# Idle matmuls in two bursts, and a re-ordered start: one change to a fused linear-attention and MLP kernel

## The chip, the cores and the metric

The kernel runs on one core of one Trainium2 chip. The metric is the device time of one execution in microseconds (us). Three runs of the kernel before took 603.48 us (median), from 602.2 to 605.39. Inside the core five engines work side by side, each with its own queue in program order: TensorE (PE in the profile; PEld is its weight load), VectorE (DVE), ScalarE (ACT), GpSimd (POOL) and SyncE (SP, which here only issues DMAs). An engine whose next instruction waits for another engine or for a DMA stands, with everything behind it in its queue.

## The reference

The attention part is a delta rule over 4 x 8 heads, 768 tokens and head size 48; its output goes through a two-layer MLP.

```
for t in range(S):
    kt, vt, bt = (k_n[:, :, t], v[:, :, t], beta[:, :, t, None])
    y[:, :, t] = np.einsum('bhd,bhde->bhe', q[:, :, t], state)
    v_old = np.einsum('bhde,bhd->bhe', state, kt)
    state = state + bt[:, :, :, None] * np.einsum('bhd,bhe->bhde', kt, vt - v_old)
x = attn_out.transpose(0, 2, 1, 3).reshape(B * S, H * D)     # 3072 x 384
h = x @ w_in                                                 # 384 x 2048
out = np.maximum(0.01 * h, h) @ w_out                        # 2048 x 384
```

## The kernel before

The 768 tokens are cut into 12 blocks of 64 tokens, each with all 32 heads. Within a block the recurrence becomes a solve with a unit triangular 64 x 64 matrix per head. VectorE inverts the two 32 x 32 halves of it by elimination (`inv` and `eliminate`, lines 394 and 399: a product into `tmp`, a subtraction from `T`, for 31 columns j). The first call (b = 0) does blocks 0 and 1 together; the call b = 1 does block 2, b = 2 block 3, and so on. TensorE joins the halves: `merge_z` (pz) and `merge_u` (pu). From block 2 on the halves reach them by way of DRAM: ScalarE copies T (line 465), SP writes `td` and `tt`, these are read back into two block-diagonal tiles `sq` (lines 477 and 481) and into `rt` (line 544). `solve` then runs in steps for both groups g of a block: load and pz, pu, `kt` (pk), `step_w` (pw, copied into `rv` by ScalarE, line 658), `step_y` (py, copied into `ys`), and `state` (pc). `columns` transposes ys (px) into the MLP's input: x in block 0, later a high part `xh` (ScalarE, line 736) and a rest `xl` (VectorE, line 739).

The MLP (`ffn`) of a block has 16 steps f: first product ph (line 761), activation gh (ScalarE, line 771), from block 1 on a second activation (line 775) and the rest gl (VectorE, line 776), and second product po (line 752), two steps f later. Block 0 uses float32 weights `cg` that are put together from raw words while it runs: `pack` and `expand` on ScalarE, `conv` and `final` (line 175) on VectorE. From block 1 on each weight is a pair w of float32r tiles, made by `cast` (ScalarE, line 182) and `lows` (VectorE, line 189).

The order of the queues comes from the order of the calls, which a scheduler may move; `behind(name)` keeps an instruction behind a marked one in its engine's queue. The main loop puts solve steps, elimination steps and weight work of the coming block between the f steps of the present one, by tables: `SV` holds the f at which the solve steps of the next block come, `IV` those of the elimination, and `work` the weight work, each entry with the mark that it stays behind. `XL` is the column of b = 1 from which the elimination stays behind xl, and `IL` the number of its steps left for that place. `WARM` puts idle matmuls (`warm`, of a constant tile `neg`, 512 columns each) behind a column of the first elimination. `lengths` multiplies v of blocks 0 and 1 by the key lengths on ScalarE (line 596); from block 2 on VectorE does so (line 647). `gram` gets the next elimination's matrix L through DRAM (`gd`, lines 313 and 343).

```
XL, IL = 20, HC - 1 - 20
WARM = {HC - 12: 16}
queue = nc.gpsimd if b > BG else nc.sync        # BG = 2: sq of blocks 2 and 3 by SP, later ones by GpSimd
gate = "xl" if b == 1 and j >= XL else None
```

## Time and profile before

| what | value |
|---|---|
| three runs | 603.48 us median, 602.2 to 605.39 |
| the profiled execution, its own time | 604.82 us |
| its span (first to last instruction) | 603.0 us |
| mean granted TensorE clock | 0.982 |
| PE busy | 561.5 us, 93% |
| DVE busy | 430.2 us, 71% |
| ACT busy | 329.9 us, 55% |
| POOL busy | 77.8 us, 13% |
| DMA | 59.69 MB, mean 99 GB/s |

Times below count from the start of the span. Busy shares are means over stages with different limits: the first 60 us have hardly any MLP work, 60 to 190 us hold blocks 0 to 2, in which the weights are still being made ready, and from there on the stages repeat. In brackets after an instruction stands the idle time of its engine just before it and what ended it ("issue": nothing that the profile shows). A granted clock of 1.00 is TensorE's 2.4 GHz, 0.50 is 1.2 GHz. Two entries of the profile for one float32 matmul of the program are its two passes.

### The profile page before, as it was taken

What the parts mean: (1) busy time and instruction counts of PE and PEld (TensorE: products, weight loads), DVE (VectorE), ACT (ScalarE), POOL (GpSimd) and SP (SyncE); (2) the same over time, 40 slices, a digit from 0 to 9 for tenths busy, and PEclk for the clock granted to TensorE, in tenths of its full rate; (3) what the DMA queues carried; (4) which work ended last, traced back from release to release, by engine and by line L of the source; (5) the groups of instructions that cost most, each with busy time, mean ns of one, the idle gap of its engine ahead of it and who ended that gap; (6) DMA issues with size and microseconds to landing.
All of it is one profiled execution on the core that took longest, in us unless ns stands there. A gap on an engine that the chain in (4) does not pass through costs nothing.

```text
span 603.0 us, 22289 instructions
## 1 busy us (share of the span) xinstructions
PE 561.5 (93%) x9106; PEld 517.5 (86%) x9106; DVE 430.2 (71%) x1942; ACT 329.9 (55%) x833; POOL 77.8 (13%) x135
## 2 busy tenths in 40 slices
PE   5278998988969999999999999999999999999996
PEld 4266776778959999999999999999999999999996
DVE  3998899778948849859859759769669579341221
ACT  3786977485455554555455446545545545454332
POOL 7000000100140040040040040130120220310100
PEclk9996998998999999999999999999999999999999
DMA  5994941345480284373381391490490450320100
GB/s 120 307 292 186 319 105 39 72 67 102 114 150 14 54 127 98 55 154 70 64 184 30 66 174 39 74 197 8 78 195 16 88 121 4 60 57 3 28 1 27
DMA packets 104423, 59.69 MB, mean 99 GB/s; under 512 B 92544, under 2 KB 93632, under 8 KB 103296
## 3 DMA queue, kind: packets, MB, share of 16 engines
q1 hardware_dynamic: 99168, 50.32, 38.3%
q0 software_dynamic: 4576, 7.22, 5.3%
q8 instruction: 72, 1.18, 0.8%
q10 hardware_dynamic: 576, 0.72, 0.5%
q14 instruction: 31, 0.25, 0.1%
HBM read 46.96 MB, written 11.27 MB: 97 GB/s over the span
## 4 chain that ended last, share of the span: by engine, by line
PE 79%; DVE 9%; ACT 5%; DMA 3%; issue 2%; SPq 1%; DVEq 0%; ACTq 0%
PE ph L761 32%; PE po L752 31%; PE py L693 3%; PE pw L656 3%; PE pg L305 3%; DVE T L399 2%; DVE tmp L394 2%; PE pk L631 2%; PE px L728 1%; PE pc L631 1%; PE pz L510 1%; PE pu L510 1%; DVE rq L322 1%; ACT cg L168 1%; DMA kx<-in_kq 1%
## 5 line engine op out<-in xcount | busy, mean ns | idle before, releaser
L752 PE MATMUL po<-w,gh 128*128 128x384 f32 x704 | 177.6, 343 | 1.8 <-ACT gh L771 1.8
L776 DVE TENSOR_TENSOR gl<-ph,gh 128x256 fp32r<-128x256 f32 x176 | 74.3, 422 | 132.2 <-ACT ph L775 129.6
L771 ACT ACTIVATE gh<-ph 128x256 fp32r<-128x256 f32 (+1 forms) x192 | 73.5, 385 | 168.0 <-PE ph L761 109.1
L761 PE MATMUL ph<-xh,w 128*128 128x256 f32 x1056 | 156.5, 284 | 0.0
L761 PEld LDWEIGHTS ph<-xh,w 128*128 128x128 f32 x1056 | 141.4, 190 | 4.1 <-issue 3.3
L752 PEld LDWEIGHTS po<-w,gh 128*128 128x128 f32 x704 | 120.5, 190 | 5.9 <-ACT gh L771 2.1
L752 PE MATMUL po<-w,gl 128*128 128x384 f32 x352 | 111.4, 337 | 1.6 <-DVE gl L776 1.6
L394 DVE TENSOR_TENSOR tmp<-T,L 128x60 f32<-128x60 f32 (+35 forms) x661 | 112.3, 205 | 0.4
L399 DVE TENSOR_TENSOR T<-T,tmp 128x60 f32<-128x60 f32 (+35 forms) x661 | 111.6, 205 | 1.0
L761 PE MATMUL ph<-xl,w 128*128 128x256 f32 x528 | 91.1, 284 | 0.0
L761 PEld LDWEIGHTS ph<-xl,w 128*128 128x128 f32 x528 | 75.3, 191 | 0.4 <-issue 0.2
L752 PEld LDWEIGHTS po<-w,gl 128*128 128x128 f32 x352 | 65.1, 188 | 2.3 <-DVE gl L776 2.3
L775 ACT ACTIVATE ph<-ph 128x256 f32<-128x256 f32 x176 | 66.9, 380 | 0.0
L477 POOL DMA_DIRECT2D sq<-tt x32 | 19.0, 596 | 276.5 <-PE ph L761 98.3
L803 POOL DMA_DIRECT2D out<-ob x44 | 23.2, 532 | 140.1 <-ACT ob L802 138.7
L322 DVE TENSOR_TENSOR rq<-pg,csb 64x256 f32<-64x256 f32 x80 | 33.8, 422 | 1.6
L642 ACT ACTIVATE rt<-pk 48x512 f32<-48x512 f32 x44 | 26.1, 593 | 10.4 <-PE pk L631 9.6
L761 PE MATMUL ph<-x,cg 128*128 128x256 f32 x96 | 25.6, 418 | 0.2 <-ACT x L733 0.2
L658 ACT COPY rv<-pw 64x384 f32<-64x384 f32 x48 | 22.8, 475 | 4.9 <-PE pw L656 3.8
L465 ACT COPY T<-T 128x512 f32<-128x512 f32 x10 | 10.8, 1076 | 25.2 <-DVE T L399 25.2
L693 PEld LDWEIGHTS py<-rv,rq 128*32 128x32 f32 x1536 | 18.8, 114 | 5.9 <-ACT rv L658 2.4
L656 PEld LDWEIGHTS pw<-rv,rt 128*32 128x32 f32 x1536 | 18.9, 114 | 5.6 <-issue 2.0
(108 smaller groups left out, 626.0 us busy)
## 6 DMA issues: line engine op xcount, KB each, us to landing
wr<-in_w_all SPq DMA_DIRECT2D x8, 1536.0 KB, 12.9
kq<-in_kqT SPq DMA_DIRECT2D x40, 192.0 KB, 5.5
rv<-in_kv SPq DMA_DIRECT2D x24, 192.0 KB, 6.4
rk<-in_kv SPq DMA_DIRECT2D x24, 192.0 KB, 6.6
rq<-in_qT SPq DMA_DIRECT2D x24, 192.0 KB, 3.4
L<-gd SPq DMA_DIRECT2D x18, 256.0 KB, 4.2
out<-ob POOLq DMA_DIRECT2D x44, 96.0 KB, 4.7
td<-T SPq DMA_DIRECT2D x20, 128.0 KB, 3.2
```

The lines of the kernel that those rows point to most:

```text
L322: nc.vector.tensor_tensor(qa[to, c, b * NPAIR:(b + 1) * NPAIR], pv[b][r, 1], tri[r].rearrange("p (o t) -> p o t", o=1).broadcast_to([C, NP ...
L394: nc.vector.tensor_tensor(tv, t[:, :, j:j + 1].broadcast_to([P, k, w]), L[:, j, j + 1:].rearrange("p (o w) -> p o w", o=1).broadcast_to([P ...
L399: mark["steps"] = mark[f"step{x}"] = nc.vector.tensor_tensor(t, t, tv, ALU.subtract).ins
L642: nc.scalar.mul(ts[g][STATE[g], c], pv[g][c * C:c * C + D].rearrange("p (y v) t -> p y v t", y=2), -1.0)
L656: nc.tensor.matmul(pv[a:a + HC, u], t[:, c, u // NPAIR, u % NPAIR, e * HC:(e + 1) * HC], v[:, c, u], start=True, stop=True)
L693: nc.tensor.matmul(pv[a:a + HC, u * D:(u + 1) * D], qa[:, c, u, e * HC:(e + 1) * HC], v[:, c, u], start=True, stop=True)
L752: i = nc.tensor.matmul(po[t][:, :DO], a[:, ts_], w, start=(f == 0 and k == 0), stop=(f == NFC - 1 and k + 1 == len(ways)))
L761: i = nc.tensor.matmul(ph, w[:, cc * P:(cc + 1) * P], a, start=(k == 0), stop=(k + 1 == len(ways)))
L771: i = nc.scalar.activation(gh, ph, AF.Prelu, alpha=0.01)
L775: i = nc.scalar.activation(ph, ph, AF.Prelu, alpha=0.01)
L776: mark["gl"] = nc.vector.tensor_tensor(gl, ph, gh.bitcast(F32), ALU.subtract).ins
L803: nc.gpsimd.dma_start(out[r0:r0 + C], ob[a:a + C])
```

## The change

- `WARM`: a burst of 28 idle matmuls behind column 16 of the first elimination and one of 12 behind column 30, in place of 16 behind column 20. A burst is tied to VectorE's progress by a matmul that reads one column of T instead of a row of it. `FILL`: two idle matmuls more behind pz of block 0, and three behind its pu. `neg` moves into a buffer of the gl tiles.
- The `sq` DMAs of block 2 go into GpSimd's queue; those of block 3 stay on SP, with the four from `tt` ahead of the four from `td`. GpSimd's DMA queue gets 2048 bytes of descriptor memory instead of 1024.
- v of block 2 is fetched a block earlier in the code and multiplied by the lengths on ScalarE, in 32 pieces (`scaled`) at f = 12 and f = 14 of block 0 and behind xh; VectorE's four multiplications of block 2 go.
- `XL` goes from 20 to 26: six columns more of block 2's elimination stand ahead of xl.
- `SV` of block 0: the last two solve steps of block 1 (py and pc) move from f = 8, 9 to f = 12, 13. `pack` 7 is put behind rt, `expand` 7 behind rv, and `lows` 3 and 4 stand together.

```diff
@@ -82,7 +82,7 @@
-    neg = st.tile([P, P], F32R, name="neg")
+    neg = sb.tile([P, TB], F32R, tag="gl", name="neg", bufs=3)[:, 0:P]
     NR = dict(k=KT_BUFS, q=Q_BUFS, t=KT_BUFS, v=2 * NGR)
@@ -186,7 +186,10 @@
         with behind("gl" if j > 4 else "dv"), behind("el0" if j > 2 else None), behind("el1" if j > 2 else None):
-            after(nc.vector.tensor_tensor(lo, g, hi.bitcast(F32), ALU.subtract))
+            d = nc.vector.tensor_tensor(lo, g, hi.bitcast(F32), ALU.subtract)
+        mark["dv"] = d.ins
+        if j < 3:
+            after(d)
         for y, part in enumerate((hi, lo)):
@@ -398,13 +401,15 @@
-    def warm(x, count):
+    def warm(count, x=None, gate=None):
         ps = ps_a.tile([P, 512], F32, tag="a", name="warm")
-        nc.tensor.matmul(ps[:, 0:HC], eye, x, start=True, stop=True)
+        if x is not None:
+            nc.tensor.matmul(ps[:, 0:1], eye, x, start=True, stop=True)
         for i in range(count):
-            nc.tensor.matmul(ps.rearrange("p (o t) -> p o t", t=P), neg,
-                             neg.rearrange("p (o t) -> p o t", o=1).broadcast_to([P, 4, P]), start=True, stop=True)
+            with behind(gate):
+                nc.tensor.matmul(ps.rearrange("p (o t) -> p o t", t=P), neg,
+                                 neg.rearrange("p (o t) -> p o t", o=1).broadcast_to([P, 4, P]), start=True, stop=True)
@@ -444,7 +449,7 @@
             if two and j in WARM:
-                warm(T[:, 0], WARM[j])
+                warm(WARM[j], T[:, 0, j:j + 1])
             if j == HC - 2:
@@ -471,13 +476,13 @@
                     A, B = square(0), square(1)
-                    queue = nc.gpsimd if b > BG else nc.sync
+                    queue = nc.sync if b == BG else nc.gpsimd
                     for k in range(4):
...
                         r = slice(v * HC, (v + 1) * HC)
-                        with behind("A" if b > BG else None):
+                        with behind("A"):
                             queue.dma_start(B[r, :, r], td[1, v::4].rearrange("l m i -> m l i"))
@@ -524,8 +529,11 @@
                     for h in range(2):
-                        nc.tensor.matmul(zv[h * 64:h * 64 + HC, u], gt[lo, u // NPAIR * GU + h * NPAIR + u % NPAIR],
+                        i = nc.tensor.matmul(zv[h * 64:h * 64 + HC, u], gt[lo, u // NPAIR * GU + h * NPAIR + u % NPAIR],
                                          t[lo, h, u // NPAIR, u % NPAIR, HC:], start=True, stop=True)
+            if not n and g:
+                mark["pz"] = i.ins
+                warm(FILL["pz"], gate="pz")
             if not g:
@@ -540,7 +548,7 @@
         for e in (1, 0):
-            with behind("L" if n > BG + 1 else None):
+            with behind("L" if n > BG + 1 else "A" if n > BG else None):
                 nc.sync.dma_start(half_of(n, g, e).rearrange("p h u i -> p (h u) i"), T[e, g * GH:(g + 1) * GH].rearrange("l m i -> m l i"))
@@ -554,7 +562,10 @@
                 for h in range(2):
-                    nc.tensor.matmul(uv[h * 64:h * 64 + HC, u], g1[:, u // NPAIR, h * NPAIR + u % NPAIR], z[r, h, u], start=True, stop=True)
+                    i = nc.tensor.matmul(uv[h * 64:h * 64 + HC, u], g1[:, u // NPAIR, h * NPAIR + u % NPAIR], z[r, h, u], start=True, stop=True)
+            if not n and g:
+                mark["pu"] = i.ins
+                warm(FILL["pu"], gate="pu")
             for h in range(2):
@@ -590,11 +601,19 @@
         for g in range(NGR):
-            v = of("v", n, g)
-            for u in range(GU):
-                for c in range(2):
+            mark["nt"] = scale(n, nt, g).ins
+
+    def scale(n, nt, g, us=range(GU), gate=None):
+        v = of("v", n, g)
+        for u in us:
+            for c in range(2):
+                with behind(gate):
                     d = nc.scalar.mul(v[DATA[g], c, u], v[DATA[g], c, u], nt[DATA[g], g, c, u:u + 1])
-        mark["nt"] = d.ins
+        return d
+
+    def scaled(n, quarters, gate):
+        for k in quarters:
+            scale(n, nts[n].rearrange("p (g h u) -> p g h u", g=NGR, h=2), k // 2, range(k % 2 * NPAIR, (k % 2 + 1) * NPAIR), gate)
@@ -604,11 +623,11 @@
             if n:
-                fetch(n, g, ("kq" if n == 1 else "kvq") if n < EARLY else "k")
+                fetch(n, g, "kq" if n < EARLY else "k")
         def ahead(g):
-            if EARLY <= n + 1 < nblk:
-                fetch(n + 1, g, "vq")
+            if 1 < n + 1 < nblk:
+                fetch(n + 1, g, "v" if n + 1 < EARLY else "vq")
@@ -639,9 +658,10 @@
                 for c in range(2):
-                    nc.scalar.mul(ts[g][STATE[g], c], pv[g][c * C:c * C + D].rearrange("p (y v) t -> p y v t", y=2), -1.0)
+                    d = nc.scalar.mul(ts[g][STATE[g], c], pv[g][c * C:c * C + D].rearrange("p (y v) t -> p y v t", y=2), -1.0)
+                mark["rt"] = d.ins
                 v, to = of("v", n, g), DATA[g]
-                for s in range(GS * (n > 1)):
+                for s in range(GS * (n > 2)):
                     us = slice(s * NPAIR, (s + 1) * NPAIR)
@@ -873,12 +893,12 @@
         8: ((final, 5), (conv, 6), (cast, 2, "h0_8"), (lows, 2)),
-        9: ((expand, 6, "h0_9"), (pack, 7, "h0_8")),
+        9: ((expand, 6, "h0_9"), (pack, 7, "rt")),
         10: ((final, 6), (conv, 7),),
-        11: ((expand, 7, "h0_11"),),
-        12: ((final, 7),),
-        13: ((cast, 3, "h0_12"),), 14: ((cast, 4, "h0_13"),), 
-        NF + 1: ((lows, 3), (cast, 5, "h1_0")), NF + 2: ((lows, 4),), NF + 3: ((cast, 6, "h1_2"),),
+        11: ((expand, 7, "rv"),),
+        12: ((final, 7), (scaled, 2, (0,), "h0_12")),
+        13: ((cast, 3, "h0_12"),), 14: ((cast, 4, "h0_13"), (scaled, 2, (1,), "h0_14")), NF: ((scaled, 2, (2, 3), "xh"),),
+        NF + 1: ((lows, 3), (lows, 4)), NF + 2: ((cast, 5, "h1_1"),), NF + 3: ((cast, 6, "h1_2"),),
         NF + 4: ((lows, 5),), NF + 5: ((cast, 7, "h1_4"),), NF + 6: ((lows, 6),), NF + 8: ((lows, 7),)}
@@ -892,13 +912,13 @@
 WEARLY, NPACK, NG = 4, 3, 5
-WARM = {HC - 12: 16}
+WARM, FILL = {HC // 2: 28, HC - 2: 12}, dict(pz=2, pu=3)
 KA = 2
 BG = 2
-XL, IL = 20, HC - 1 - 20
+XL, IL = 26, HC - 1 - 26
 IV, GG = ((9, 16), (6, 17), (2, 12), (2, 12)), ((2, 4), (1, 2))
 G4 = (0, 1), (13, 14), (12, 13)
-SV = (1, 2, 4, 5, 7, 8, 9), (4, 6, 7, 9, 11, 12), (2, 4, 5, 7, 9, 10), (3, 3, 5, 6, 8, 10, 11)
+SV = (1, 2, 4, 5, 7, 12, 13), (4, 6, 7, 9, 11, 12), (2, 4, 5, 7, 9, 10), (3, 3, 5, 6, 8, 10, 11)
 PD, FB = 2, 4
@@ -956,7 +976,7 @@
     arrs, nblk = _layout(inputs)
-    nc = _bacc.Bacc("TRN2", target_bir_lowering=False, num_devices=1, dynamic_dma_scratch_size=1024)
+    nc = _bacc.Bacc("TRN2", target_bir_lowering=False, num_devices=1, dynamic_dma_scratch_size=2048)
     arrays, args = {}, []
```

ScalarE's queue around py of block 1 in block 0 (gh_10 to gh_15 are the activations of its MLP steps, rv the copies of pw and pc, cg and w weight work, nt the lengths), before:

```order
L771 ACTIVATE gh_11_1570<-ph_73 128x256
L168 CAST cg_1473<-cg_1473 128x1536
L658 COPY rv_86<-pw_0_1310 64x384 x2
L658 COPY rv_87<-pw_1_1345 64x384 x2
L695 COPY ys_0_1431<-py_0_1398 128x384
L695 COPY ys_1_1466<-py_1_1433 128x384
L670 COPY rv_84<-pc_0_1475 48x384 x2
L670 COPY rv_85<-pc_1_1494 48x384 x2
L771 ACTIVATE gh_12_1599<-ph_72 128x256
```

and now:

```order
L791 ACTIVATE gh_11_1509<-ph_73 128x256
L678 COPY rv_86<-pw_0_1345 64x384 x2
L678 COPY rv_87<-pw_1_1380 64x384 x2
L168 CAST cg_1438<-cg_1438 128x1536
L791 ACTIVATE gh_12_1544<-ph_72 128x256
L611 ACTIVATE rv_84<-rv_84,nt_1458 64x48 x8
L791 ACTIVATE gh_13_1651<-ph_72 128x256
L182 CAST w_1655<-cg_1035 128x1536
L182 CAST w_1729<-cg_1094 128x1536
L715 COPY ys_0_1590<-py_0_1557 128x384
L715 COPY ys_1_1625<-py_1_1592 128x384
```

The copies of pw now stand ahead of the weight cast, and two activations, eight multiplications of v and two weight casts stand between them and the copies of py.

ScalarE's queue where block 1's MLP begins (ob are block 0's results on their way out, T the copy for tt of block 2), before:

```order
L736 CAST xh_2_1718<-px_1_1705 128x256
L802 COPY ob_0_1728<-po_0_984 128x384
L802 COPY ob_1_1732<-po_1_985 128x384
L771 ACTIVATE gh_0_1756<-ph_72 128x256
L775 ACTIVATE ph_72<-ph_72 128x256
L182 CAST w_1852<-cg_1245 128x1536
L771 ACTIVATE gh_1_1846<-ph_72 128x256
```

and now:

```order
L756 CAST xh_2_1805<-px_1_1792 128x256
L611 ACTIVATE rv_85<-rv_85,nt_1458 64x48 x16
L822 COPY ob_0_1815<-po_0_1017 128x384
L822 COPY ob_1_1819<-po_1_1018 128x384
L470 COPY T_1440<-T_1440 128x16x32
L791 ACTIVATE gh_0_1843<-ph_72 128x256
L795 ACTIVATE ph_72<-ph_72 128x256
L507 ACTIVATE sq_1901<-csb 128x1024
L507 ACTIVATE sq_1903<-csb 128x1024
L312 COPY gs_0_1928<-pg_0_0_1930 128x256
```

Sixteen multiplications and the copy of T now stand ahead of gh_0, and the zeroing of both sq tiles ahead of gh_1; a weight cast has moved behind gh_1.

SP's queue around block 2's sq (gd and L belong to block 3's elimination), before:

```order
L471 DMA tt_1829<-T_1513 1024x1x16 x2
L313 DMA gd_1861<-gs_0_1862 32x8x32 x3
L477 DMA sq_1834<-tt_1829 32x8x32 x4
L313 DMA gd_1861<-gs_0_1862 32x8x32
L313 DMA gd_1861<-gs_1_1892 32x8x32
L481 DMA sq_1836<-td_1828 32x8x32 x4
L313 DMA gd_1861<-gs_1_1892 32x8x32 x3
L544 DMA rt_82<-td_1828 32x16x32 x2
L343 DMA L_1860<-gd_1861 64x1024 x2
L544 DMA rt_83<-td_1828 32x16x32 x2
```

and now:

```order
L476 DMA tt_1896<-T_1440 1024x1x16 x2
L552 DMA rt_82<-td_1895 32x16x32 x2
L552 DMA rt_83<-td_1895 32x16x32 x2
L316 DMA gd_1927<-gs_0_1928 32x8x32 x4
L316 DMA gd_1927<-gs_1_1958 32x8x32 x4
L346 DMA L_1926<-gd_1927 64x1024 x2
```

The eight sq DMAs are gone from here, and rt has moved ahead of gd and L.

## Rows read from the trace of the kernel before

**Rows 1.** The page: span, and the chain that ended last, by engine.
```profile
span 603.0 us, 22289 instructions
...
PE 79%; DVE 9%; ACT 5%; DMA 3%; issue 2%; SPq 1%; DVEq 0%; ACTq 0%
```

**Rows 2.** Windows: busy us by engine, with counts; granted clock, DMA share, GB/s.
```profile
45.00:50.00 5.00, 3.04 (x140) 2.67 (x131) 4.82 (x8) 2.23 (x5) 0.00 (x0) 0.50 0.05 16
55.00:60.00 5.00, 5.00 (x78) 4.15 (x77) 3.05 (x4) 2.83 (x5) 0.00 (x0) 0.88 1.00 425
95.00:100.00 5.00, 2.78 (x10) 2.21 (x11) 4.77 (x16) 3.36 (x5) 0.00 (x0) 0.72 0.02 5
140.00:145.00 5.00, 3.82 (x66) 3.71 (x67) 4.39 (x17) 2.14 (x4) 0.00 (x0) 0.66 0.67 142
200.00:250.00 50.00, 50.00 (x798) 47.57 (x786) 39.36 (x213) 25.12 (x68) 6.80 (x12) 1.00 0.49 92
```

**Rows 3.** PE's timeline, blocks 0 to 2: start, us, instruction [idle before, releaser].
```profile
97.22 0.38 PE L693 MATMUL py<-rv,rq 128*32 128x48 f32 x4 [2.22 <-ACT rv L658]
...
124.74 0.62 PE L752 MATMUL po<-w,gl 128*128 128x384 f32 x2 [0.90 <-DVE gl L776]
...
129.98 0.65 PE L510 MATMUL pz<-sq,gm 128*32 128x128 f32 x16 [1.42 <-DMA sq<-tt]
...
141.18 1.62 PE L631 MATMUL pk<-rt,rk 64*48 64x64 f32 x58 [2.05 <-DMA rt<-td]
...
168.80 0.97 PE L752 MATMUL po<-w,gh 128*128 128x384 f32 x4 [1.83 <-ACT gh L771]
...
180.45 0.64 PE L510 MATMUL pz<-sq,gm 128*32 128x128 f32 x16 [2.65 <-DMA sq<-tt]
```

**Rows 4.** PE's timeline in the first 60 us.
```profile
31.55 5.88 PE L406 MATMUL warm<-neg 128*128 128x512 f32 x16
...
47.10 1.42 PE L656 MATMUL pw<-rv,rt 128*32 128x48 f32 x59 [1.86 <-issue]
...
53.90 4.00 PE L761 MATMUL ph<-x,cg 128*128 128x256 f32 x12 [0.25 <-ACT x L733]
...
59.40 2.86 PE L761 MATMUL ph<-x,cg 128*128 128x256 f32 x12
```

**Rows 5.** VectorE's timeline where block 0's MLP begins.
```profile
56.33 1.75 DVE L175 SCALAR_TENSOR_TENSOR cg<-wr,cg 128x1536 uint32<-128x1536 uint32 x1
```

**Rows 6.** VectorE's timeline around xl of block 1.
```profile
113.62 1.09 DVE L739 TENSOR_TENSOR xl<-px,xh 128x256 fp32r<-128x256 f32 x3 [3.54 <-ACT xh L736]
...
120.93 3.42 DVE L189 TENSOR_TENSOR w<-cg,w 128x1536 fp32r<-128x1536 f32 x2
```

**Rows 7.** ScalarE's timeline: v of block 1, the first gh of block 1, T of block 3.
```profile
27.69 6.70 ACT L596 ACTIVATE rv<-rv,nt 64x48 f32<-64x48 f32 x29
...
118.90 0.39 ACT L771 ACTIVATE gh<-ph 128x256 fp32r<-128x256 f32 x1 [2.62 <-PE ph L761]
...
167.49 1.05 ACT L465 COPY T<-T 128x512 f32<-128x512 f32 x1 [4.91 <-DVE T L399]
```

**Rows 8.** SP's timeline: how long its queue issues block 2's DMAs.
```profile
126.60 1.78 SPq L477 DMA_DIRECT2D sq<-tt  x4
...
129.47 2.89 SPq L481 DMA_DIRECT2D sq<-td  x4
...
136.28 1.11 SPq L544 DMA_DIRECT2D rt<-td  x2
```

**Rows 9.** VectorE's timeline where block 3's elimination begins.
```profile
140.20 0.19 DVE L362 TENSOR_SCALAR sr<-L 128x32 uint32<-128x32 uint32 x1 [2.40 <-DMA L<-gd]
140.42 1.61 DVE L647 TENSOR_TENSOR rv<-rv,nt 64x384 f32<-64x384 f32 x3
```

**Rows 10.** POOL's timeline: its fourth gd DMA in block 2.
```profile
167.48 0.58 POOL L313 DMA_DIRECT2D gd<-gs  x1 [3.70 <-issue]
```

**Rows 11.** DMA issues by line: count, KB each, median us to landing.
```profile
sq<-td POOLq DMA_DIRECT2D x32, 32.0 KB, 4.7
```

## The prediction

> **What bounds the kernel now.** I read the page first. The chain that ended last lies on PE for 79% of the span [rows 1], and in the repeating part from 200 to 250, PE is busy for 50.00 us of 50 at full clock [rows 2]. There nothing that another engine does faster can help. So what this change can win lies ahead of that part, and I went through PE's timeline for the places where it stood. From the first MLP product on there are seven, six of them in [rows 3]: 2.22 + 0.90 + 1.42 + 2.05 + 1.83 + 2.65 = 11.07 us, after which PE never stands again. The windows show the second loss, the clock. It stands at 0.50 in 45 to 50, comes back inside 55 to 60 (0.88), and falls twice more, to 0.72 in 95 to 100 and 0.66 in 140 to 145 [rows 2]; these two stretches hold the stops at 97.22 and 141.18 [rows 3]. A clock of 0.72 over 5 us is 1.4 us of full-speed work lost, one of 0.66 is 1.7 us.
>
> **The change part by part.** Sums are against the profiled execution (604.82 us, span 603.0), which lies 1.3 us above the median of 603.48. I take the difference from the median.
>
> *Start.* The chain pz, pu, pw, py, px runs at 1.2 GHz, and the first products still do: twelve take 4.00 us at 53.90, and twelve take 2.86 at 59.40, at 2.4 GHz [rows 4]. The extra idle matmuls are work that could keep the clock up. But PE isn't alone here. The second pair of first products (59.40) needs the weights that VectorE has ready at 56.33 + 1.75 = 58.08 [rows 5], and VectorE's own queue before that isn't shortened. So even a perfect clock wins at most 59.40 - 58.08 = 1.3 us. On the other side stand five idle matmuls between pz and pw, at 5.88/16 = 0.37 us each [rows 4], so 1.8 us if the clock falls anyway; the 1.86 us for which PE stood at 47.10 on nothing that the profile shows [rows 4] may hide that. The second burst (12 x 0.37 = 4.4 us, or less at full clock) falls into the transposition and the copy ahead of pz, so I cost it at nothing. Between -1.8 and +1.3 I take +0.9, since the clock would be high already from the first burst.
>
> *py of block 1.* PE stood 2.22 us there for ScalarE's copies rv, which came behind a weight cast. The new order has rv ahead of the cast, and py four f steps later. The stop goes, and with it the 1.4 us of clock: +3.6, bounds 0 (another copy is late instead) and 3.6.
>
> *xl of block 1.* Between xl's end (114.71) and the weight rest at 120.93 VectorE did eleven columns of the elimination [rows 6], at most (120.93 - 114.71)/11 = 0.57 us each, so six cost up to 3.4 us. Before, VectorE stood 3.54 us for xh ahead of xl [rows 6]: the six columns fill that hole and the inverse ends earlier by about as much. But PE is earlier by 3.6 + 0.9 as well, so xh comes earlier, the hole closes, and xl is late by something. I take -0.6; bounds 0 and -3.4.
>
> *v times lengths on ScalarE.* 29 pieces took 6.70 us [rows 7], so 32 cost 7.4. The first sixteen lie beside PE's MLP work in block 0. The other sixteen (3.7 us) stand between xh and gh_0 of block 1, with the copy of T behind them. Before, ScalarE stood 2.62 us for ph ahead of gh_0 [rows 7]. With PE 4 us earlier that cover is gone, and gh_1 comes behind both zeroings of sq as well. I take -3.7. Bounds: -1.1 (3.7 less the 2.62, if the cover stays) and -6.0 (3.7 and 2.3 for a T that isn't finished when its copy comes up).
>
> *sq of block 2 in GpSimd's queue.* SP spent 1.78 + 2.89 = 4.67 us on these eight DMAs, ahead of rt, whose last pair was issued only at 136.28 [rows 8]; pk waited for it until 141.18. In the new queue rt is issued right behind tt. Together with the earlier end of the inverse this takes away the waits of gl (0.90), pz (1.42) and pk (2.05) and the second clock drop (1.7): +6.1, bounds 0 and 6.1. The Trainium skill speaks against it ("DMA: Bandwidth & Descriptors", section "Issuing engines are not separate DMA queues"): DMAs of all queues end on the same sixteen engines, and a second queue saves only the time to issue them, which is usually small beside the transfer. By that alone pk would gain nothing and the sum would lose about 3.8. Here the trace disagrees: those 4.67 us of issue are what rt stands behind, and the DMA engines are busy only 0.67 of that stretch [rows 2, 8].
>
> *Block 2.* VectorE loses the four multiplications of v, three of which (1.61 us) stand inside the beginning of block 3's elimination, which itself waited 2.40 us for L [rows 9]; gd and L now come earlier in SP's queue. The copy of T for block 3, for which ScalarE stood 4.91 us [rows 7] and PE then 1.83, goes behind two more activations. pz of block 3 waited 2.65 us for sq. Of 1.83 + 2.65 = 4.5 us I count 2.5: PE is now ahead by some 6 us when it gets here, and the elimination has to come forward as much before any of the 4.5 is won. Bounds -1.0 and +4.5.
>
> The rest is set at nothing: neg in a gl buffer, and more descriptor memory in the repeating part, where PE doesn't wait.
>
> Sum: 0.9 + 3.6 - 0.6 - 3.7 + 6.1 + 2.5 = 8.8 us. 604.82 - 8.8 = 596.0 for an execution like the profiled one, **603.48 - 8.8 = 594.7 us** for the median. All good ends give 1.3 + 3.6 - 1.1 + 6.1 + 4.5 = 14.4 (589.1); all bad ones -1.8 - 3.4 - 6.0 - 1.0 = -12.2 (615.7).
>
> **The rivals.** (1) *GpSimd's queue is late.* In block 2 GpSimd's fourth gd DMA stood for 3.70 us on nothing that the profile shows, and started at 167.48 [rows 10]; VectorE's last elimination step let ScalarE's copy of T go at 167.49 [rows 7]. So GpSimd seems held while VectorE eliminates, and by a further 4.7 us to landing (median of sq from td, [rows 11]) pz and pu would get sq late. For it: the sq DMAs come right behind the inverse, where VectorE does 3.42 us of weight rests [rows 6]. Against it: no eliminations run then. Price 3.7 us: 598.4. The Trainium skill has the mechanism ("SBUF — State Buffer", section "SBUF: two separate sides"): GpSimd writes the descriptors of its DMAs itself, through a port that it shares with VectorE, and stands while VectorE has it. By that rule the time is that of this rival; the row on the fourth gd DMA agrees with it.
>
> (2) *ScalarE becomes the bound.* The activations of block 1 wait for 7.4 us more ScalarE work, its term goes to -6.0, and py finds another late copy (0 instead of 3.6): 8.8 - 2.3 - 3.6 = 2.9 us won, 600.6, which is no change. For it: both stretches have ScalarE close behind PE. Against it: the casts of weights 5 and later were moved away from there.
>
> (3) *Slower: the copy of T.* It now stands ahead of gh_0 in a queue that keeps its order. If block 2's inverse ends no earlier than before (its end is near 120.9, where the weight rests begin [rows 6]), ScalarE stands until then, gh_0 starts near 122 instead of 118.90 [rows 7], two zeroings stand ahead of gh_1, and PE waits some 4.5 us with another clock drop (1.7). The sq term then gives nothing, since its waits stay. With the start, py and xl as above that is 0.9 + 3.6 - 0.6 - 4.5 - 1.7 = -2.3, and with block 2 at its lower bound (-1.0) it is -3.3: 606.8. The trace shows this very thing once: 4.91 us of ScalarE for T, then 1.83 of PE. It decides from the point where the inverse doesn't win the 3.54 us; six columns in the hole speak against that.
>
> **How the numbers follow.** Chances: the sum 0.62, GpSimd late 0.18, ScalarE the bound 0.13, the copy of T 0.07. A measurement of this kernel tells about 0.5% (3.0 us) from no change, so faster means below 600.5. The first two cases lie below it but for their upper ends, the third on its edge. That gives faster 0.83, same 0.11, slower 0.06. The range runs from the sum of the good ends (589) to just past the third case (601.5); what lies outside is the fourth case and a few hundredths on either side.
>
> **What would show it.** Right: a granted clock of 1.00 from the first burst through 55; no stop at py, and none at pk; the clock at 1.00 in block 0's end and block 2's solve; the first ph pair no earlier than VectorE's weights. Wrong: the clock still at 0.50 through pw and py (start term); PE waiting for gh_0 or gh_1 of block 1, with ScalarE standing before T (third rival); GpSimd's sq DMAs with idle time marked issue between them, and pz waiting for them (first rival). If pz of block 3 waits longer than 2.65 us, the elimination did not come forward and the last term is too large.

## The result, and the profile after

| | kernel before | changed kernel |
|---|---|---|
| median of 6 runs | 605.19 us (602.2 to 605.79) | 596.06 us (594.78 to 600.29) |
| ratio | | 0.9875, 95% interval 0.9838 to 0.9912 |
| the profiled execution | 604.82 us, span 603.0 | 594.78 us, span 593.0 |
| mean granted clock, profiled execution | 0.982 | 0.995 |
| the same, timed executions | 0.975 to 0.991, median 0.984 (66, from the sets below) | 0.990 to 0.995, median 0.993 (6) |

Faster by 1.25%, some 7.6 us by the ratio (5.3 to 9.8 by its interval); the two medians lie 9.1 us apart. The forecast was a gain of 8.8 us and a time of 594.7 us. The difference of the median clocks, 0.009 of some 600 us, is 5.4 us of full-speed work, but not all of it is time won: in the profiled pair the clock stood at 0.50 near the start for 13.7 us before and for 3.4 us now, which is 5.1 us of full-speed work, and PE's lead behind it is 1.0 us (first row of the table of leads below). The page of the changed kernel, answering to [rows 1] (span; chain that ended last, by engine):

```profile
span 593.0 us, 22382 instructions
...
PE 78%; DVE 13%; ACT 4%; issue 2%; DMA 1%; DVEq 0%; ACTq 0%
```

The windows of [rows 2] after the change (the number behind the counts is the granted clock):

```profile
45.00:50.00 5.00, 3.68 (x163) 2.73 (x162) 4.85 (x8) 2.33 (x5) 0.00 (x0) 0.77 0.03 8
55.00:60.00 5.00, 4.78 (x80) 4.01 (x79) 3.24 (x5) 3.98 (x5) 0.00 (x0) 1.00 0.97 406
95.00:100.00 5.00, 5.00 (x141) 3.33 (x139) 4.91 (x29) 4.72 (x13) 0.00 (x0) 1.00 0.20 51
140.00:145.00 5.00, 5.00 (x152) 4.68 (x151) 4.99 (x37) 2.77 (x7) 0.00 (x0) 1.00 0.04 8
200.00:250.00 50.00, 50.00 (x771) 47.61 (x770) 37.85 (x182) 27.42 (x76) 7.21 (x13) 1.00 0.52 96
```

The two later falls of the clock are gone, and the one at the start is shorter: 0.77 instead of 0.50 in 45 to 50. PE's timeline, at the places of [rows 3] and [rows 4] and at the new stops (start, us, instruction [idle before, releaser]):

```profile
58.36 2.86 PE L781 MATMUL ph<-x,cg 128*128 128x256 f32 x12 [0.22 <-DVE wr L131]
...
97.12 1.58 PE L713 MATMUL py<-rv,rq 128*32 128x48 f32 x128
...
112.88 1.05 PE L781 MATMUL ph<-xl,w 128*128 128x256 f32 x5 [1.09 <-DVE xl L759]
...
119.35 0.44 PE L772 MATMUL po<-w,gl 128*128 128x384 f32 x1 [0.72 <-DVE gl L796]
...
120.92 0.97 PE L772 MATMUL po<-w,gh 128*128 128x384 f32 x4 [0.61 <-ACT gh L791]
...
126.91 0.64 PE L515 MATMUL pz<-sq,gm 128*32 128x128 f32 x16 [1.41 <-DMA sq<-tt]
...
135.88 1.12 PE L650 MATMUL pk<-rt,rk 64*48 64x64 f32 x64
...
161.11 0.97 PE L772 MATMUL po<-w,gh 128*128 128x384 f32 x4 [0.68 <-ACT gh L791]
...
163.93 0.62 PE L772 MATMUL po<-w,gl 128*128 128x384 f32 x2 [0.70 <-DVE gl L796]
...
170.04 0.65 PE L515 MATMUL pz<-sq,gm 128*32 128x128 f32 x16
```

py and pk stand no more, nor does pz of block 3 (the last line, 2.65 us before). pz of block 2 stands as long as before (1.41, before 1.42), and xl, gl and gh in block 1 have stops of 1.09, 0.72 and 0.61 us.

How far PE is ahead of the kernel before, at the same matmul in both profiles:

| matmul | before | after | ahead |
|---|---|---|---|
| first products, second pair of block 0 | 59.40 | 58.36 | 1.0 |
| first products of block 0 behind py and pc | 107.13 | 101.69 | 5.4 |
| first product from xl, block 1 | 116.97 | 112.88 | 4.1 |
| pz of block 2 | 129.98 | 126.91 | 3.1 |
| py of block 2 | 152.20 | 145.13 | 7.1 |
| pz of block 3 | 180.45 | 170.04 | 10.4 |
| end of the span | 603.0 | 593.0 | 10.0 |

### The profile page after: what moved, and what is told of

Same layout as the page of the kernel before. It is cut to its first block, busy times and chain, and to the rows that moved or that the text cites. A ratio compares the mean times of both kernels' runs of the same rounds, so it can differ in the third digit from the quotient of the medians.

```text
span 593.0 us, 22382 instructions
## 1 busy us (share of the span) xinstructions
PE 563.6 (95%) x9137; PEld 518.3 (87%) x9137; DVE 428.0 (72%) x1938; ACT 336.9 (57%) x865; POOL 82.0 (14%) x143
## 4 chain that ended last, share of the span: by engine, by line
PE 78%; DVE 13%; ACT 4%; issue 2%; DMA 1%; DVEq 0%; ACTq 0%
PE ph L781 31%; PE po L772 30%; DVE tmp L397 3%; DVE T L402 3%; PE pw L676 3%; PE py L713 2%; PE warm L411 2%; PE pg L308 2%; PE pk L650 2%; PE pc L650 1%; DVE w L189 1%; DVE rq L325 1%; PE px L748 1%; PE pz L515 1%; PE pu L515 1%
## 5 line engine op out<-in xcount | busy, mean ns | idle before, releaser
L482 POOL DMA_DIRECT2D sq<-tt x36 | 21.2, 594 | 301.2 <-DMA tt<-T 184.2
L772 PE MATMUL po<-cg,gh 128*128 128x384 f32 x64 | 23.1, 494 | 0.0
L781 PE MATMUL ph<-x,cg 128*128 128x256 f32 x96 | 22.3, 382 | 0.6 <-ACT x L753 0.4
L611 ACT ACTIVATE rv<-rv,nt 64x48 f32<-64x48 f32 x96 | 22.2, 318 | 0.1
```

The costliest lines, as they stand in the source:

```text
L611: d = nc.scalar.mul(v[DATA[g], c, u], v[DATA[g], c, u], nt[DATA[g], g, c, u:u + 1])
L772: i = nc.tensor.matmul(po[t][:, :DO], a[:, ts_], w, start=(f == 0 and k == 0), stop=(f == NFC - 1 and k + 1 == len(ways)))
L781: i = nc.tensor.matmul(ph, w[:, cc * P:(cc + 1) * P], a, start=(k == 0), stop=(k + 1 == len(ways)))
```

## The experiments

Each time stands as a ratio to the kernel before, measured on the same chip, with its 95% interval; the changed kernel has 0.9875, and 0.001 is 0.6 us. The intervals of u_start, c_start_llast, u_len, u_ring, a_ring and a_warm lie clear of the changed kernel's, u_py's overlaps it by 0.0002, and the others overlap it more; a difference of two ratios is given in us from their middles, and is uncertain by 2 to 3 us. The last two columns turned out to matter: the stop of pz of block 3, and how long the four sq DMAs from tt of block 3 took to land (the median of the four, and the one issued last, which pz waits for).

| kernel | ratio | stop at pz of block 3, us | sq, us to landing: median, last |
|---|---|---|---|
| before | 1 | 2.65 | 3.1, 4.7 |
| changed | 0.9875 (0.9838 to 0.9912) | none | 2.2, 2.4 |
| u_start: old idle matmuls | 0.9949 (0.9920 to 0.9978) | 3.04 | 3.9, 3.9 |
| c_start_llast: the same, L behind out | 0.9967 (0.9951 to 0.9982) | 4.09 | 4.3, 4.8 |
| u_py: py, pc at their old place | 0.9939 (0.9910 to 0.9969) | 1.19 | 2.3, 3.9 |
| u_sq: sq of block 2 by SP | 0.9898 (0.9861 to 0.9935) | none | 2.2, 2.2 |
| u_len: v times lengths on VectorE | 0.9974 (0.9945 to 1.0003) | 4.04 | 4.4, 3.9 |
| u_xl: XL = 20 | 0.9890 (0.9839 to 0.9942) | none | 2.3, 2.5 |
| u_ring: descriptor memory 1024 | 0.9943 (0.9916 to 0.9970) | 2.94 | 2.5, 5.2 |
| c_lfirst: L ahead of out | 0.9927 (0.9899 to 0.9955) | 1.40 | 4.0, 4.2 |
| i_b: new order in block 1 | 0.9910 (0.9872 to 0.9948) | 2.68 | 2.4, 5.1 |
| i_c: XL = 20, L on SP behind sq | 0.9906 (0.9870 to 0.9942) | none | 2.2, 2.2 |
| a_ring: before, memory 2048 | 0.9982 (0.9950 to 1.0014) | none | 3.5, 3.2 |
| a_warm: before, new idle matmuls | 1.0070 (1.0036 to 1.0105) | 5.03 | 5.6, 5.2 |

### One part undone at a time

```
u_start   -WARM, FILL = {HC // 2: 28, HC - 2: 12}, dict(pz=2, pu=3)   +WARM, FILL = {HC - 12: 16}, dict(pz=0, pu=0)
```

> The changed kernel with the old idle matmuls (16 behind column 20, none behind pz and pu). Theory A, the terms add up: the first product of the second pair starts about 1.0 us later (near 59.4 instead of 58.36), the clock is at 0.50 for some 10 us more, and the whole is 1.0 us slower than the changed kernel (near 597). Theory B, VectorE's inverse of block 2 sets the time at which TensorE gets through the beginning of block 1: the 1.0 us is absorbed in TensorE's waits for xl (1.09), gl (0.72) and pz (1.41), which shrink by as much, and the whole is within 0.3 us of the changed kernel (near 596). The price on record, 0.9 us, holds in both at 60 us, and at the end only in A.

Neither. At 60 us nothing is lost: the second pair starts at 58.12, earlier than in the changed kernel. PE keeps level with it up to 161 us, and loses 5 us at one place, pz of block 3, where the clock falls as well (0.50 for 6.8 us from 171.81):

```profile
172.64 1.08 PE L515 MATMUL pz<-sq,gm 128*32 128x128 f32 x16 [3.04 <-DMA sq<-tt]
```

The scheduler had ordered later work anew: in GpSimd's queue the two L DMAs of block 4 (166.61) now stand ahead of the four out DMAs (167.70), which they follow in the changed kernel.

```
u_py      -SV = (1, 2, 4, 5, 7, 12, 13), ...   +SV = (1, 2, 4, 5, 7, 8, 9), ...   (pack 7 and expand 7 behind their old marks)
```

> The changed kernel with py and pc of block 1 back at f = 8 and 9 of block 0, and the pack and expand of weights 7 behind their old marks. TensorE should stand again some 2 us before py for ScalarE's copies rv, with a clock drop behind it. Theory A: the whole is 3.6 to 4.4 us slower than the changed kernel (near 600). Theory B: as far as the waits for xl, gl, gh and pz (1.09 + 0.72 + 0.61 + 1.41 = 3.8 us) are set by VectorE and the way of T through DRAM, they close first, and the whole is only 0.5 to 1.5 us slower (near 597).

Theory A's size: 0.0064 more than the changed kernel is 3.9 us. py stood again, and the clock fell behind it (0.50 for 3.4 us from 100.68):

```profile
100.67 0.38 PE L713 MATMUL py<-rv,rq 128*32 128x48 f32 x4 [2.67 <-ACT rv L678]
```

That the size is this stop alone isn't shown: the profiled execution is the slowest of ten, and in it PE stood 2.88 us at pz of block 2 too, with another fall of the clock behind it.

```
u_sq      -queue = nc.sync if b == BG else nc.gpsimd   +queue = nc.sync if b <= BG else nc.gpsimd
```

> The changed kernel with the sq DMAs of block 2 back in SP's queue. Theory: pz comes at about the same time (SP issues four in 1.8 us, GpSimd in 2.35), but gd and L of block 3 stand behind 4.7 us more of issue in SP's queue, so that block 3's elimination begins some 4 us later, and TensorE's stops at the beginning of block 2's MLP (0.68 and 0.70) grow: 2 to 4 us slower than the changed kernel. Rival, by the rule that queues share the same DMA engines and a second queue saves little: within 0.5 us of the changed kernel. Second rival, GpSimd's queue is the late one: pz's wait of 1.41 us goes and the whole is 1 us faster.

In time it can't be told from the changed kernel (the intervals overlap), but its trace shows the theory's chain: SP's queue issued L of block 3 at 131.79 instead of 128.64, and VectorE stood for it at an instruction that started at 133.74 without a wait in the changed kernel. First VectorE, then ScalarE:

```profile
136.64 0.19 DVE L365 TENSOR_SCALAR sr<-L 128x32 uint32<-128x32 uint32 x1 [3.53 <-DMA L<-gd]
```

```profile
162.35 1.05 ACT L470 COPY T<-T 128x512 f32<-128x512 f32 x1 [3.74 <-DVE T L402]
```

T came 2.6 us later (159.79 in the changed kernel), and PE was 2.2 us behind at block 3's pu. The stops of 0.68 and 0.70 did not grow (0.65 and 0.71); new ones of 0.66 and 1.00 us for gl came in block 2, and 0.95 us at pg.

The second rival holds in part: with SP's queue pz of block 2 started 0.7 us earlier and stood half as long. And pk of block 2 does not stand here either, though sq is on SP again, because three of the four rt DMAs are issued ahead of sq. PE, then SP's queue:

```profile
126.20 0.65 PE L515 MATMUL pz<-sq,gm 128*32 128x128 f32 x16 [0.70 <-DMA sq<-tt]
...
134.94 1.12 PE L650 MATMUL pk<-rt,rk 64*48 64x64 f32 x64
```

```profile
121.05 1.39 SPq L552 DMA_DIRECT2D rt<-td  x3
122.61 1.84 SPq L482 DMA_DIRECT2D sq<-tt  x4
```

```
u_len     -for s in range(GS * (n > 2)):   +for s in range(GS * (n > 1)):   (and no scaled in work)
```

> The changed kernel with v of block 2 multiplied by the lengths on VectorE again (four multiplications behind gl), and ScalarE's 32 pieces left out. The price on record: ScalarE's pieces cost 3.7 us at the beginning of block 1, so that without them gh_0 comes earlier and the whole is 1.5 to 3.7 us faster. Theory: gh_0 waits for T (ScalarE stood 2.45 us for it behind the pieces), so the pieces cost nothing there; the four multiplications (2.2 us on VectorE) come back ahead of block 3's elimination, and the whole is 0 to 2 us slower.

The price on record falls, sign and all: without ScalarE's 32 pieces the kernel is 6.0 us slower, more than the theory said as well. In the changed kernel ScalarE did the last sixteen ahead of the copy of T and then still stood for T; without them it stands longer for the same T. The changed kernel, then this one:

```profile
108.75 3.72 ACT L611 ACTIVATE rv<-rv,nt 64x48 f32<-64x48 f32 x16
...
115.66 1.11 ACT L470 COPY T<-T 128x512 f32<-128x512 f32 x1 [2.45 <-DVE T L402]
```

```profile
116.89 1.12 ACT L470 COPY T<-T 128x512 f32<-128x512 f32 x1 [4.71 <-DVE T L402]
```

On VectorE the four multiplications stand at the very beginning of block 3's elimination, and pz of block 3 pays (sq moved beside L there, 4.4 us in the table):

```profile
135.68 2.08 DVE L667 TENSOR_TENSOR rv<-rv,nt 64x384 f32<-64x384 f32 x4
```

```profile
177.13 0.64 PE L515 MATMUL pz<-sq,gm 128*32 128x128 f32 x16 [4.04 <-DMA sq<-tt]
```

```
u_xl      -XL, IL = 26, HC - 1 - 26   +XL, IL = 20, HC - 1 - 20
```

> The changed kernel with XL back at 20. VectorE is busy without a hole up to xl in the changed kernel's profile, so that the inverse of block 2 should end at the same time (near 115.5) wherever xl stands. Theory: the wait for xl (1.09 us) goes, but gl_0, which stands behind the inverse and 3.42 us of weight rests, comes at the same time as before, so that TensorE waits there instead: within 0.5 us of the changed kernel in block 1, where the copy of T now stands later on ScalarE (behind gh_1 and a weight cast) and may cost 1 us more at pz. The price on record for the six columns, 0.6 us, would make it 0.6 us faster; the gain that was the reason for them (an inverse that ends 3.5 us earlier) would make it slower by 2 us or more.

xl starts at 109.50 instead of 112.40 and its wait goes; VectorE's inverse ends at 116.2 instead of 115.5, two gl among its last columns. PE is 2 us ahead of the changed kernel at 176 us, but the four executions spread from 592.83 to 599.44 us, and in time the two aren't told apart. The six columns brought no earlier inverse.

### What holds pz of block 3

Two of these five, u_start and u_len, lost most of their time at pz of block 3, where none of the theories had looked. In the changed kernel the last of its four sq DMAs from tt landed 0.4 us before PE arrived. What differed was the two L DMAs of block 4 (256 KB each), which GpSimd issues.

```
c_lfirst        out DMAs of block 1: +with behind("kq" if n == 1 else None):     (kq marks L of block 4)
c_start_llast   u_start, and L of block 4 issued in the code after the out DMAs, +with behind("out")
```

> The changed kernel with one difference: in GpSimd's queue the two L DMAs of block 4 (256 KB each) stand ahead of the four out DMAs of block 1 instead of behind them, as they did in the kernel before and in the run with the old idle matmuls. Theory: L then moves while sq of block 3 comes in, sq lands 1.5 to 2 us later, pz of block 3 waits 2 to 3 us as it did in both of those profiles, and the clock falls behind it: 2 to 5 us slower than the changed kernel (598 to 601). Rival: what made pz of block 3 wait is when T is ready, and the order in GpSimd's queue is of no account: within 1 us of the changed kernel (near 596).

> The changed kernel with the old idle matmuls, as in the first run, but with block 4's L DMAs held behind the out DMAs in GpSimd's queue. The first run lost some 4 us, and all of it in its profile at pz of block 3. Theory: that was a changed order of these DMAs, not the idle matmuls; with the order of the changed kernel the time comes back to 596 to 597.5, and the idle matmuls are worth the 0 to 1 us that they show at 60 us. Rival: the clock at the start costs the 4 us (by one way or another), and the time stays near 600.5.

The first holds in kind, though its interval just overlaps the changed kernel's: 3.1 us slower, the sq DMAs took 4.0 instead of 2.2 us, and pz stood, for less than the 2 to 3 us that were expected. GpSimd's queue in the changed kernel and in this one:

```profile
155.28 4.03 POOL L316 DMA_DIRECT2D gd<-gs  x7 [27.77 <-ACT gs L312]
161.38 0.58 POOL L316 DMA_DIRECT2D gd<-gs  x1 [2.08 <-DMA gd<-gs]
165.67 2.17 POOL L823 DMA_DIRECT2D out<-ob  x4 [3.71 <-ACT ob L822]
167.89 1.19 POOL L346 DMA_DIRECT2D L<-gd  x2
```

```profile
167.31 1.10 POOL L346 DMA_DIRECT2D L<-gd  x2 [3.06 <-DMA gd<-gs]
168.40 2.07 POOL L824 DMA_DIRECT2D out<-ob  x4
```

```profile
173.64 0.60 PE L515 MATMUL pz<-sq,gm 128*32 128x128 f32 x13 [1.40 <-DMA sq<-tt]
```

The second falls: with L behind out the time did not come back (601 us), and pz stood 4.09 us. In that profile, as in u_start's, sq was issued only from 167.3 and 167.2 on (165.75 in the changed kernel), so that L, behind out or not, moved beside it. The order in the queue isn't the cause by itself; what counts is whether L is under way when the last of the four sq DMAs is. The DMA lines (issuing queue, count, KB each, median us to landing) of the changed kernel and of the slowest experiment, a_warm, show the two cases:

```profile
L<-gd POOLq DMA_DIRECT2D x2, 256.0 KB, 4.8
...
sq<-tt SPq DMA_DIRECT2D x4, 32.0 KB, 2.2
```

```profile
L<-gd POOLq DMA_DIRECT2D x2, 256.0 KB, 5.3
...
sq<-tt SPq DMA_DIRECT2D x4, 32.0 KB, 5.6
```

A median of four can hide it, since pz waits for the last. In the changed kernel, u_sq and u_xl, L was issued 0.5 to 0.9 us after the fourth sq DMA, which landed in 2.2 to 2.5 us, and pz did not stand. In u_ring, u_py and i_b, L came 0.4 to 0.6 us after it: three landed in 1.6 to 2.5 us and the fourth in 3.9 to 5.2, and pz stood. In all others but i_c, L was issued ahead of the fourth, which took 3.2 to 5.2 us; pz stood in all of them but a_ring, where PE came late enough. In u_ring, the DMAs issued from 172.6 to 173.2 us, with the first L and the fourth sq:

```profile
L<-gd POOLq DMA_DIRECT2D x1, 256.0 KB, 4.4
...
sq<-tt SPq DMA_DIRECT2D x1, 32.0 KB, 5.2
```

```
u_ring   -dynamic_dma_scratch_size=2048   +dynamic_dma_scratch_size=1024
a_ring   the kernel before: -dynamic_dma_scratch_size=1024   +dynamic_dma_scratch_size=2048   (neg in a gl buffer, for room)
```

> The changed kernel with 1024 bytes of descriptor memory for GpSimd's DMA queue instead of 2048; every queue's order stays as it is. Theory: with 1024 only three DMAs of 32 KB are under way at a time and each further one is issued 0.3 us after an earlier one has landed (before: the fourth gd at 167.48, after the first had landed at 167.14); so the fourth sq from tt of block 2 is issued near 125.4 instead of 124.62 and pz of block 2 waits about 0.8 us longer, and the gd DMAs of block 4 go out until 165 or 166 instead of 161.4: 1 to 3 us slower than the changed kernel (597 to 599). Rival, as the prediction had it: the memory is of no account, and GpSimd was held by VectorE's elimination: no difference (596), and the gaps between the gd DMAs stay as they are with 2048.

> The kernel before with 2048 bytes of descriptor memory (and the idle matmuls' tile in a gl buffer, to make room), and nothing else; every queue's order stays as it is. Theory: the gd DMAs of block 4 go out seven in a row from 162 to 166 instead of one by one until 172, although VectorE eliminates as before; L follows some 4 us earlier and no longer moves while sq of block 3 comes in, and the stop of 2.65 us at pz of block 3 shrinks: 1 to 3 us faster than the kernel before. Rival: GpSimd is held by VectorE, the fourth gd still stands until 167.5, and the time doesn't change.

These two change no queue's order. u_ring is 4.1 us slower than the changed kernel, more than expected; its profiled execution is the slowest of ten, so only its waits are read. GpSimd's queue with 1024 in the changed kernel, and with 2048 in the kernel before (compare [rows 10]):

```profile
160.24 1.74 POOL L316 DMA_DIRECT2D gd<-gs  x3 [28.55 <-ACT gs L312]
166.10 1.78 POOL L316 DMA_DIRECT2D gd<-gs  x3 [4.12 <-issue]
169.36 0.58 POOL L316 DMA_DIRECT2D gd<-gs  x1 [1.48 <-issue]
170.31 0.58 POOL L316 DMA_DIRECT2D gd<-gs  x1 [0.37 <-issue]
```

```profile
163.47 4.08 POOL L313 DMA_DIRECT2D gd<-gs  x7 [43.12 <-ACT gs L309]
169.49 0.58 POOL L313 DMA_DIRECT2D gd<-gs  x1 [1.95 <-issue]
172.64 1.09 POOL L343 DMA_DIRECT2D L<-gd  x2 [2.57 <-DMA gd<-gs]
```

With 1024 three go and the fourth stands until the first has landed: 160.24 + 5.6 us to landing is 165.8, and the fourth starts at 166.10. With 2048 seven go in a row, while VectorE is busy 4.35 of 4.50 us (163 to 167.5), most of it with the elimination, and the eighth (169.49) stands until the first has landed (169.17). So it was the memory, not VectorE, that held GpSimd. In u_ring it held sq of block 2 too:

```profile
130.32 1.02 PE L515 MATMUL pz<-sq,gm 128*32 128x128 f32 x16 [2.35 <-DMA sq<-tt]
```

0.94 us more than the 1.41 of the changed kernel (0.8 was expected), with a fall of the clock behind it. In a_ring L goes out 2.1 us earlier than before and pz of block 3 doesn't stand: there PE makes up 2.6 us against the kernel before. L still moves beside sq, but from the start of T's copy to the landing of the last sq it takes 10.6 us instead of 12.9. In time that is 0.9982, and the interval reaches 1: the trace shows a gain, the times don't.

```
a_warm   the kernel before with the new warm, +WARM, FILL = {HC // 2: 28, HC - 2: 12}, dict(pz=2, pu=3)
```

> The kernel before with the new idle matmuls alone (28 and 12 in two bursts, two behind pz and three behind pu). Price on record: 0.9 us faster than the kernel before. What the profiles so far say against it: the second pair of first products started at 58.1 to 62.2 us with the new idle matmuls (seven profiles) and at 57.9 to 59.4 with the old (three), so that no gain shows: within 0.5 us of the kernel before, unless the order of later work, which the scheduler makes anew, moves the time either way by 1 to 4 us (as it did in the run with the old idle matmuls).

Slower by 0.7%. At 60 us it is 0.9 us ahead of the kernel before, just the price on record, and at the first products of 172.09 us (175.51 before) 3.4 us ahead. All of it is lost at one instruction and the fall of the clock there (0.50 for 6.8 us from 177.05):

```profile
180.10 1.08 PE L512 MATMUL pz<-sq,gm 128*32 128x128 f32 x16 [5.03 <-DMA sq<-tt]
```

At pk of block 3 it is 0.6 us behind (189.79, before 189.21), and in this profile 2.4 us at the end, 0.8 of them in a later stop (276.17). The copy of T of block 3 came no earlier than before (168.35, before 167.49), and sq moved beside L. Neither side of the expectation had the place; the scheduler's new order of later work is the third possibility that it named.

### Two attempts at a better version

```
i_b   XL = 21; copy of T of block 2 +with behind("h1_1"); lows 3, 4 behind gl; casts 5, 6 a step later; SV[1] (4, 6, 7, 9, ...) -> (5, 6, 8, 9, ...)
i_c   XL = 20; L of block 4: nc.gpsimd -> nc.sync, +with behind("A")     (A marks sq of block 3)
```

> An attempt at a better version: xl behind column 20, the copy of T of block 2 behind gh_1 of block 1, the weight rests 3 and 4 behind gl_1, the weight casts 5 and 6 one step later, and pz of block 2 one step later (f = 5), pk at 8. If TensorE's four waits in block 1 (1.09, 0.72, 0.61, 1.41 = 3.8 us) are matters of order, they go and the whole is 1 to 3 us faster than the changed kernel (593 to 595). If they are what VectorE's inverse of block 2 and then of block 3 allow, the time that is won is waited for at the beginning of block 2's MLP and the whole stays within 1 us (near 596).

> An attempt at a better version: the changed kernel with XL = 20 (whose profile had 5.5 us of stops on TensorE from 45 us on instead of 8.6, and one execution of 592.83), and with the two L DMAs of block 4 in SP's queue behind sq of block 3, where they can't take the DMA engines while sq comes in. If pz of block 3 is a race between T's way through DRAM and the other transfers, the slow executions of XL = 20 (599.4) go and the whole is at 592 to 595, 1 to 4 us faster than the changed kernel. If not, it stays near 596.6; if SP's queue is then too long, rt of block 3 comes late, pk of block 3 waits, and it is 1 to 2 us slower.

Neither beats the changed kernel. i_b's four waits in block 1 shrank, PE was 3.4 us ahead at 120 us, and at pz of block 3 it stood 2.68 us. That is the second outcome in time, but not for its reason: T came 1.2 us earlier than in the changed kernel, and the fourth sq DMA took 5.1 us beside L. i_c did what it says, sq landed in 2.2 us and pz of block 3 never stood, but its median is 596.9 us; in its profile PE stood for a gl and for pk of block 3 instead (1.28 and 0.54 us).

## Why the prediction was right, and where its steps weren't

The time was forecast within 1.4 us, and the stops at py and pk went, with the falls of the clock behind them, as it said. The sum held partly by luck: one of its terms had the wrong sign, another was put down to the wrong edit, a third isn't shown to have a cause, and an edit that matters was set at nothing.

- *Start, 0.9.* 1.0 in the pair of profiles, and VectorE was the next to be waited for, as said (0.22 us at 58.36). But the sign on record, a clock of 1.00 up to 55, did not come (0.50 from 43.9 to 47.3), and that the idle matmuls bring the gain isn't shown. Over all 14 profiles the second pair starts at 58.1 to 62.2 us with the new ones (ten) and at 57.9 to 61.7 with the old (four); the medians are 58.9 and 58.8. How long the clock stays at 0.50 there differs from profile to profile: with the new ones from 3.4 us (the changed kernel, u_len) to 17.1 (u_py), with the old from 6.8 (u_start) to 17.1 (a_ring).
- *py, 3.6.* Measured 4.4 in the lead of PE, and 3.9 us when undone alone. Stop and clock, as worked out; the fall lasted 3.4 us from 97.20, past the window that was read, so it cost 1.7 and not 1.4.
- *xl, -0.6.* A wait of 1.09 us, a size within its bounds. The reason given (the columns fill a hole, the inverse ends earlier) isn't borne out: in u_xl the inverse ended at the same time but for two gl.
- *v times lengths, -3.7.* The failed step. "ScalarE stood 2.62 us for ph ahead of gh_0 ... that cover is gone" took the wrong cover: T, not ph, came last there, and the pieces lay in that wait. The gain on VectorE (2.08 us less at the beginning of block 3's elimination) was in the list, but as part of 2.5; when the edit is undone, the kernel is 6.0 us slower.
- *sq in GpSimd's queue, +6.1.* PE's lead grew by 4.0 from pz of block 2 to py of block 2 (pk's 2.05 and the clock), because rt was issued early, as worked out. But the second queue isn't what brings it: in u_sq, with sq on SP, three of the four rt DMAs are issued as early and pk doesn't stand. Which edit moved rt ahead in SP's queue wasn't tried. pz's 1.42 stayed (1.41), and with GpSimd's queue it started 0.7 us later than with SP's, which is the first rival's direction at a fifth of its price. The gl and gh stops of block 1 cost 1.0 of the lead. Together with the -3.7, 2.4 was forecast for what measured 3.0, so the errors cancelled: that is luck. The DMA share of 0.67 in the prediction belongs to 140 to 145; from 126.6 to 137.4, when SP issued these DMAs, it was 0.43, so the argument there stands. Of the Trainium skill's rule ("DMA: Bandwidth & Descriptors", section "Issuing engines are not separate DMA queues") that a second queue saves only issue time, u_sq's trace says: it is all that is saved, but 3.15 us of it stood ahead of L of block 3.
- *Block 2, 2.5.* 3.3 from py of block 2 to pz of block 3, of which 0.4 is lost again by the end. T came as much earlier as PE did (7.7 us), which is what the prediction asked of the elimination; the stop of 2.65 went because T's path from its copy to the last sq shrank from 12.9 to 9.8 us. That cause was missed. "The rest is set at nothing: ... more descriptor memory in the repeating part, where PE doesn't wait" left out that sq of block 2 and gd and L of block 4 come through it before that part begins: undone, it costs 4.1 us, and alone in the kernel before it shortens T's path by 2.3.

The first rival's mechanism (GpSimd held while VectorE eliminates) is refuted by a_ring. The Trainium skill ("SBUF — State Buffer", section "SBUF: two separate sides") was read too widely there: it has VectorE lock the shared port in a two-port mode, and with two SBUF inputs only against a GpSimd instruction that reads SBUF. The 4.12 us in u_ring's queue and the 3.70 us of [rows 10] are explained by the memory without it. The second and third rivals didn't come: ScalarE stood 2.45 us for T ahead of gh_0, but PE waited only 0.61 us for a gh in block 1, not the third rival's 4.5.

Why the parts don't add up: six edits undone one at a time (u_start, u_py, u_sq, u_len, u_xl, u_ring) cost 4.5 + 3.9 + 1.4 + 6.0 + 0.9 + 4.1 = 20.8 us, and all of them together only 7.6. pz of block 3 is where PE's path meets T's path through DRAM, and whichever is later sets the time. An edit that wins on one path alone wins nothing there (a_warm), and undoing any one of several can lose the same stop, mostly with a fall of the clock. From T's copy to the last sq it took 9.8 us in the changed kernel, 13.3 in u_start and 14.3 in c_start_llast. Of the 3.4 and 4.5 us more, 1.4 and 2.4 are sq beside L; the other 2 lie ahead of sq, where td landed in 5.6 us instead of 3.5. Why it landed later there was not tried, and stays open. So does how much of the changed kernel's time is luck: in its profile the last sq landed 0.4 us ahead of PE, and L was issued 0.7 us after that sq.

## What to carry to other kernels

When two paths join at one instruction, price an edit by what it does to the later one, and look for the join before adding up terms: here the sum was right and half its terms weren't. GpSimd's queue, standing on nothing that the profile shows and going on 0.3 us after an earlier DMA of its own had landed, was out of room for descriptors; compare starts with landings before blaming another engine. Keep a large transfer that nobody waits for away from a small one that PE waits for (i_c did, and pz of block 3 did not stand, though its time was no better). When an instruction waits for several DMAs, read the landing of the last, not their median.

## What the runs showed that was not expected

- GpSimd's DMA queue has three 32 KB DMAs of this shape under way with 1024 bytes of descriptor memory and seven with 2048; the next is issued 0.3 us after the first has landed (u_ring, a_ring).
- Four 32 KB DMAs from SP landed in 2.2 us (median) beside four of 96 KB from GpSimd (the changed kernel, u_sq, i_c), and in 3.9 to 5.6 us beside two of 256 KB (u_start, c_lfirst, u_len, a_warm).
- One stop can cost twice: at pz of block 3 the clock stayed at 1.00 after 2.65 us in the kernel before, but stood at 0.50 for 3.4 us after 2.68 us in i_b (1.7 us more of full-speed work), and for 6.8 us around the 3.04 us in u_start (3.4 us more).
